# Retention and a gated feed-forward layer on one core: loads queued ahead of transposes, and fences by halves of the outputs

## The chip, the cores and the metric

The kernel runs on one core of one Trainium2 chip. The metric is the device time of one execution in microseconds (us); lower is better. The core has five engines that run side by side: TensorE (PE; its weight loads are listed apart as PEld), VectorE (DVE), ScalarE (ACT), GpSimd (POOL) and SyncE (SP), which here issues nearly all DMAs. TensorE multiplies a moving operand by weights that were loaded before and writes to PSUM, eight banks of accumulators; ScalarE and VectorE bring the results from there to SBUF.

## The reference

For each of 8 batches and 8 heads (sequence 576, head width 64) it computes retention, which is attention without softmax, with a decay that depends on the distance. The heads are laid side by side to 512 columns, and 4608 rows go through a two-layer network with a gate.

```python
scores = scale * np.matmul(q, k.transpose(0, 1, 3, 2))
Dmat = np.where(rel >= 0, gamma[:, None, None] ** rel[None, :, :], 0.0)
ret = scores * Dmat[None, :, :, :]
attn = np.matmul(ret, v)                      # (8, 8, 576, 64)
...
x = attn.transpose(0, 2, 1, 3).reshape(4608, 512)
h = x @ w_in                                  # 512 -> 2048
g = h * (1.0 / (1.0 + np.exp(-beta * h)))
out = g @ w_out                               # 2048 -> 512
```

The decay is separable, so the kernel puts it into q and v as factors (`gq`, `gv`), and only a triangular mask is left. The inputs are random normal numbers.

## The kernel before

**Blocks.** The first 512 rows of each batch form a block (m = 0 to 7); the last 64 rows of all eight batches form a ninth block, "the tails". A block goes up (L714: 16 groups of 4 matmuls with 512 columns, 512 to 2048 wide), through the gate (L718, L719, L721) and down: blocks 0 to 3 with plain matmuls (`down`, L824), blocks 4 to 8 with seven products in place of eight (`seven_mm`, L751).

**Retention of a batch, from batch 2 on.** The 512 rows are taken in half tiles of 64 rows. `scores` (L550) multiplies k by q inside the half tiles and masks the result with VectorE into R. States are sums of k times v over a half tile (`four_states`, L523); `fold` (L528) adds them up and casts them to bf16 into seven tiles `sbq`. `outputs4` (L589) multiplies v by R into four PSUM tiles O4[x, y], 64 matmuls. `crosses4` (L607) adds what earlier half tiles contribute: q times the sums `sbq[e - 1]` for e = 1 to 7, for each of four head pairs p = 2y + pp, and for two heads j in each: 56 matmuls into the same four PSUM tiles. Then `out` (L626) copies O4 to `xT`, the input of the block's up matmuls. `both4` is outputs and crosses together. The tails have the same steps in `tail_scores`, `tail_outputs`, `tail_crosses` (L647 to L698), with 64 outputs and 64 crosses. `XB`, 2, is the first batch done in this way; batches 0 and 1 use larger tiles.

**Small matmuls on TensorE.** All of these work on 64x64 tiles: half of the array's rows and half of its columns, so four quarters. The row half is that of the partitions the weights and the moving operand lie in (`row_d(j)` or `half(x)`, rows 0 to 63 or 64 to 127), the column half that of the PSUM partitions written. In a cross the row half is j and the column half j ^ y. `paired` (L493) takes two lists and issues an entry of each in turn, so that the stream alternates between row halves. `mm` (L498, the matmul is L499) issues all of them.

**The fence.** Within a bank, accumulating matmuls from different row halves must not run together. The crosses therefore come in two parts: first those in which row half j writes the tiles x = j, whose outputs came from the same row half, and then those with x = 1 - j. Before the second part starts, all outputs have to be done: `fence` (L504) has ScalarE make a tiny copy (`fenced`, L505) that waits for the last output matmul, and the first cross of the second part waits for that copy (`after`). In batches 3 to 6 the states of the next batch's first four half tiles (32 matmuls, `ahead`) stand between the two parts.

**Order.** Nothing is scheduled automatically. `fill` is a list of units, mostly one group of four 512-column matmuls each. `streams` are lists of (place, step), and `merged` (L844) issues each step just before the fill unit of that number. `base[n]` is the place of the first unit of block n, `d0` that of the first down unit, `u1` that of block 1's first up unit. A step's instructions go to their engines' queues in this order, each engine works its queue in order, and a step at a wrong place waits there with all that stands behind it.

**Loads and transposes.** SyncE's queue holds q loads (L86, two per batch), k and v loads (`load_kv`: L100, L102, L105, one tile of 128 rows each; L105 in two halves), the DMA transposes of q (`x_q`), of k (`x_k`) and of the tails (all L362), and the stores of the results (L790, L815, L837; L815 are block 0's and 1's, held back and sent by `release`). `pre_q` and `pre` have GpSimd scale q and v and cast k to bf16; a transpose waits for that. A batch has four k/v tiles c = 0 to 3; `x_k(b, 0)` turns the keys of c = 0 and 1, `x_k(b, 1)` those of c = 2 and 3. `kvn` has six buffers, `qs` one. `pair_prep` (L965) says where the loads and the preparation of a pair of tiles stand: for batches 3 to 7 it puts loads of c = 2 and 3 at `at - 28` and `at - 26` (batch 3: `at - 25.4`, `at - 25.3`), among the transposes of the same batch; for batch 2 the streams at L944 to L959 do.

Of the kernel before, what the change touches and what calls it, by code (L numbers as in the profile page):

```python
# [19 lines left out]
def kernel(  # L20
# [15 lines left out]
    P = 128  # L36
# [4 lines left out]
    CB = MB // P  # L41
    PC = P // CB
    TL = S - MB
# [241 lines left out]
    def F(f, *a):  # L285
        return lambda: f(*a)  # L286
# [199 lines left out]
    def row_d(j):  # L486
        return slice(j * D, (j + 1) * D)
# [101 lines left out]
    def outputs4(b):  # L589

        i0 = b * CB
        O4, opened = new_O4(i0, [P, 2, CB, 2 * PC]), set()
        R = batch[b]["R"]

        def one(x, y, cc, pp, kind, hh):
            p, c = 2 * y + pp, 2 * cc + x
            w = cc * PC + kind * PC // 2
            mm(O4[x, y][row_d(hh), pp, :, w:w + PC // 2], live[i0 + tile_of(c, kind)]["vn"][half(x), 2 * p + hh, :],
               R[cc][half(x), hh ^ y, kind, p, :].rearrange("k (i s) -> k i s", i=CB), start=(x, y, hh) not in opened, stop=False)
            opened.add((x, y, hh))  # L600

        for y in range(2):
            paired(*[[F(one, x, y, cc, pp, kind, hh ^ x) for cc in range(2) for pp in range(2) for kind in range(2)
                      for hh in range(2)] for x in range(2)])
        batch[b]["O4"] = O4, fence()

    def crosses4(b, later=None):  # L607

        i0 = b * CB
        O4, after = batch[b]["O4"]  # L610

        def cross(j, e, y, pp, after):
            p, c, kind = 2 * y + pp, e // 2, e % 2
            w = c // 2 * PC + kind * PC // 2
            mm(O4[c % 2, y][row_d(j ^ y), pp, :, w:w + PC // 2], sbq[e - 1][row_d(j), p, :],
               q_cols(i0 + c, row_d(j), p, kind)[0], after=after)

        def crosses(j, x, after=None):
            return [F(cross, j, e, y, pp, after) for e in range(1, 2 * CB) if e // 2 % 2 == x for pp in range(2) for y in range(2)]

        ahead, bank = ([], []), None
        if b < B - 1 and b != XB:
            bank = state_banks()
            ahead = four_states(b + 1, 0, bank)
        paired(*[crosses(j, j) + ahead[j] + crosses(j, 1 - j, None if j else after) for j in range(2)])
        def out(n, x, y, O):  # L626
            to = xt(b)[:, 2 * y:2 * y + 2].rearrange("k p i (c x s) -> k (p i) c x s", c=2, x=2)[:, :, :, x, :]
            e = nc.scalar.copy if n == 1 or b > XB and n % 2 or later is not None else nc.vector.tensor_copy
            e(to, O[:].rearrange("k p i (c s) -> k (p i) c s", c=2))  # L629

        outs = [F(out, n, x, y, O) for n, ((x, y), O) in enumerate(O4.items())]
        if later is not None:
            casts = []
            if bank:
                fold(b + 1, 0, bank, casts=casts, by=nc.scalar.copy)
            later += outs + casts
            return
        for f in outs:
            f()
        if bank:  # L640
            fold(b + 1, 0, bank)
# [23 lines left out]

    def tail_outputs(i0):

        O4, opened, R = new_O4(i0, [P, 2, NT, TL]), set(), live[i0]["R"]

        def one(x, y, t, pp, hh):  # L670
            p = 2 * y + pp
            mm(O4[x, y][row_d(hh), pp, t, :], live[i0 + t]["vn"][half(x), 2 * p + hh, :],
               R[t // 2][half(x), hh ^ y, t % 2 * HP + p, :], start=(x, y, hh) not in opened, stop=False)
            opened.add((x, y, hh))

        for y in range(2):
            paired(*[[F(one, x, y, t, pp, hh ^ x) for t in range(NT) for pp in range(2) for hh in range(2)]
                     for x in range(2)])
        live[i0]["O4"] = O4, fence()

    def tail_crosses(i0, later):

        O4, after = live[i0]["O4"]

        def cross(j, x, t, y, pp, after):
            p = 2 * y + pp
            mm(O4[x, y][row_d(j ^ y), pp, t, :], ends[2 * t + x][row_d(j), p, :], live[i0 + t]["qkT"][row_d(j), 0, p, half(x)],
               after=after)

        for own in range(2):  # L690
            paired(*[[F(cross, j, j ^ own, t, y, pp, after if own else None) for t in range(NT) for pp in range(2) for y in range(2)]
                     for j in range(2)])
        def out(x, y, O):
            for r in range(2):
                to = xt(B)[:, 2 * y:2 * y + 2].rearrange("k p (a r) (s l x) -> k (p a) r l x s", r=2, l=2, x=2)[:, :, r, :, x, :]
                nc.scalar.copy(to, O[:].rearrange("k p (a l) (r s) -> k (p a) r l s", l=2, r=2)[:, :, r])

        later += [F(out, x, y, O) for (x, y), O in O4.items()]  # L698
# [239 lines left out]
    def second(i):  # L938
        for f in (a_O, lambda j: a_cross(j, False), a_x):
# [7 lines left out]
               [(d0 - 4 + 3.3 * g, F(cast_w_out, g)) for g in range(WG)],  # L947
               [(10.3, F(load_q, 1))] + [(10.3, F(load_kv, CB + n, (j,))) for n, j in keys_first],
               [(10.4, F(load_q, 2))] + [(10.4, F(load_kv, 2 * CB + n)) for n in range(2)],
               [(d0 + 8.6, F(load_kv, 2 * CB + 2)), (d0 + 12.6, F(x_q, XB, 0)), (d0 + 12.7, F(x_q, XB, 1)),  # L950
                (d0 + 13.6, F(x_k, XB, 0)), (d0 + 13.8, F(load_kv, 2 * CB + 3)),
                (base[2] - 4.5, F(release, 4)), (base[2] + 8, F(release, 4))],
               [(d0 + 7, F(pre_q, 1, n)) for n in range(4)] + [(d0 + 12.5, F(pre_q, XB, n)) for n in range(4)] + [(d0 + 11.6, F(t_q, 1, 0)), (d0 + 12.6, F(t_q, 1, 1))],
               [(d0 + 8, F(pre, 4, (0,))), (d0 + 8, F(pre, 5, (0,))), (d0 + 9, F(pre, 4, (1,))), (d0 + 9, F(pre, 5, (1,))),
# [10 lines left out]
    def pair_prep(i, at):  # L965
        b, c = seq[i]
        if b is None:
            if c:
                return [(at - 27, F(load_tail, c)), (at - 20, F(load_tail, c + 1)), (at - 17.5, F(pre, i)),
                        (at - 12, F(pre, i + 1)), (at - 12, F(x_tail, i)), (at - 9.5, F(x_tail, i + 1))]  # L970
            return [(at - 31, F(load_tail, c)), (at - 21.5, F(pre, i)), (at - 21, F(load_tail, c + 1)),
                    (at - 13, F(pre, i + 1)), (at - 12, F(x_tail, i)), (at - 9.5, F(x_tail, i + 1))]
        n, st = full.index(i), []
        if b == XB:
            if c == 0:
                return [(d0 + 13, F(pre, i + x, (0,))) for x in range(2)] + \
                       [(d0 + 14, F(pre, i + x, (1,))) for x in range(2)]
            return [(u1 + 8 + x / 2, F(pre, i + x)) for x in range(2)]
        if c == 0:
            st += [(at - 30, F(load_q, b, (0,)))] + ([(at - 30, F(x_k, XB, 1))] if b == XB + 1 else [])  # L980
            st += [(at - 30, F(load_q, b, (1,)))] + [(at - 20 + x, F(pre_q, b, x)) for x in range(4)]
            st += [(at - 14 + 1.5 * x, F(x_q, b, x)) for x in range(2)]
            return st + [(at - 28, F(load_kv, n)), (at - 26, F(load_kv, n + 1)), (at - 16, F(pre, i)),
                         (at - 15, F(pre, i + 1)), (at - 11.5, F(x_k, b, c // 2))]
        turned_at = asked[b + 1] - 30.1
        st += [(turned_at - 0.4 + 0.1 * x, F(pre, i + x, (0,))) for x in range(2)]
        st += [(turned_at, F(x_k, b, c // 2))] + [(turned_at + 0.1 + 0.1 * x, F(pre, i + x, (1,))) for x in range(2)]
        early = b == XB + 1
        return st + [(at - (25.4 if early else 28), F(load_kv, n)), (at - (25.3 if early else 26), F(load_kv, n + 1))]

    def span(a, n, by=1.0):
        return [a + by * x for x in range(n)]
# [30 lines left out]
    for n in range(1, B):  # L1023
# [3 lines left out]
        b, t = n + 1, base[n]  # L1027
        t0 = t + lead.get(n, 0)
        if n == 1:
            at = [t + 17, base[b] - 8.9]  # L1030
        elif n < SB:
            at = [t + 3, t + 18]
        else:
            at = [t0 - 13, t0 + 2] if n < B - 1 else [t0 - 9.5, t0 - 2.5]
# [5 lines left out]
            streams.append([(at[0], F(group1, b, (0,))), (at[1], F(group1, b, (1,))), (at[1] + 4.4, F(both4, b))])  # L1040
        elif n < SB:
            streams.append([(t + 16, F(first_states, b))] * (b == XB + 1) +
                           [(t + 19, F(group1, b, (0, 1))), (t + 25.9, F(both4, b))])
        elif n == B - 1:
            outs = []
            streams.append([(t0, F(tail_scores, take[0])), (t + 13, F(both_tails, take[0], outs))] +
                           queued([t + 16.3, t + 17.6, t + 20.5, t + 22.5], outs))
        else:
            rest, outs = [], []
            t0 -= behind[n]  # L1050
            streams.append([(t0, F(scores, b, (0, 1), rest))] + queued([t0 + 0.1, t0 + 0.9, t0 + 0.9, t0 + 1.8, t0 + 2.6] + span(t0 + 3.4, 4, 0.9), rest))
            by = t + 14.5 if n == SB else t + 12.8
            streams.append([(by, F(both4, b, outs))] + queued([t + 16.3] * 4 + [t + 17.3, t + 18.3, t + 20.3, t + 20.4][:4 if n < B - 2 else 0], outs))
# [32 lines left out]
```

## Time and profile before

| | |
|---|---|
| three runs | 291.69, 292.61, 293.07 us; median 292.61 |
| the profiled execution | 292.13 us, span 290.4 us, granted TensorE clock 1.00 |
| TensorE matmuls, busy | 280.4 us, 97% of the span |
| DVE, ACT, POOL, busy | 168.4, 172.6, 119.6 us |
| small matmuls L499: sc, st, O | 0.19 to 0.20 us mean length each, overlapping |
| DMA transposes L362 | 28 issues; qT lands 5.4 us after issue, kT 3.7 us (medians) |
| k and v loads | 88 issues, 128 or 256 KB; median 3.7 to 5.8 us to landing |

How to read it: the busy share of an engine tells where there is room, and TensorE has next to none. The length of a single small matmul is its latency, many are in flight at once, so their pace is read from the starts: a group's length less the last one's own, divided by the number of steps. A chain of waits is followed back from the end of the program, at each step to what released it; "issue" is time in which the engine waited for nothing that the profile shows.

### The profile page before, as it was taken

What the parts mean: (1) busy time and instruction counts of PE and PEld (TensorE: products, weight loads), DVE (VectorE), ACT (ScalarE), POOL (GpSimd) and SP (SyncE); (2) the same over time, 40 slices, a digit from 0 to 9 for tenths busy, and PEclk for the clock granted to TensorE, in tenths of its full rate; (3) what the DMA queues carried; (4) which work ended last, traced back from release to release, by engine and by line L of the source; (5) the groups of instructions that cost most, each with busy time, mean ns of one, the idle gap of its engine ahead of it and who ended that gap; (6) DMA issues with size and microseconds to landing.
All of it is one profiled execution on the core that took longest, in us unless ns stands there. A gap on an engine that the chain in (4) does not pass through costs nothing.

```text
span 290.4 us, 8109 instructions
## 1 busy us (share of the span) xinstructions
PE 280.4 (97%) x3357; PEld 171.3 (59%) x3385; DVE 168.4 (58%) x314; ACT 172.6 (59%) x306; POOL 119.6 (41%) x219
## 2 busy tenths in 40 slices
PE   8899999999999999999999999999999999999995
PEld 6554446864544454445554885578557845784584
DVE  6563556804673375405538976986597555642673
ACT  4676646686639895882257725772576156837730
POOL 4765206782565473337349245615389000000000
PEclk9999999999999999999999999999999999999999
DMA  7999999999999999599999979996789130003004
GB/s 211 218 341 386 387 275 227 253 187 194 214 153 258 251 277 189 139 254 175 193 257 217 170 113 257 260 162 142 234 192 169 41 148 3 2 29 116 2 2 142
DMA packets 128884, 54.01 MB, mean 186 GB/s; under 512 B 110400, under 2 KB 121680, under 8 KB 128848
## 3 DMA queue, kind: packets, MB, share of 16 engines
q1 hardware_dynamic: 128816, 53.49, 82.9%
q8 instruction: 26, 0.43, 0.7%
q14 instruction: 10, 0.08, 0.1%
q10 hardware_dynamic: 32, 0.01, 0.0%
HBM read 36.71 MB, written 9.44 MB: 159 GB/s over the span
## 4 chain that ended last, share of the span: by engine, by line
PE 86%; SPq 6%; DMA 4%; issue 1%; DVE 1%; POOL 1%; ACT 0%; DVEq 0%; POOLq 0%
PE ph L714 39%; PE po L824 16%; PE U L751 9%; PE Z L751 6%; PE W L751 6%; SPq L100 3%; PE O L499 3%; DMA wt<-in_moe_w_in_dram 3%; PE ph L806 2%; DMA kvn<-in_k_dram 2%; PE sc L499 1%; PE st L499 1%; SPq L198 1%; PE sc L403 0%; DVE sum L535 0%
## 5 line engine op out<-in xcount | busy, mean ns | idle before, releaser
L714 PE MATMUL ph<-xT,w_in_sb 128*128 128x512 bf16 (+1 forms) x544 | 113.9, 363 | 1.4 <-issue 0.6
L721 ACT ACTIVATE gT<-ph,beta_sb 128x512 bf16<-128x512 f32 (+1 forms) x100 | 63.6, 644 | 42.1 <-PE ph L714 41.2
L714 PEld LDWEIGHTS <-w_in_sb 128*128 128x128 bf16 x560 | 53.5, 98 | 55.7 <-POOL w_in_sb L206 0.9
L824 PE MATMUL po<-w_out_sb,gT 128*128 128x512 bf16 x246 | 56.2, 379 | 1.2 <-issue 1.0
L354 POOL CAST kn<-kvn 128x128 bf16<-128x128 f32 (+2 forms) x80 | 30.2, 411 | 58.1 <-DMA kvn<-in_k_dram 57.7
L751 PEld LDWEIGHTS <-sa 128*128 128x128 bf16 x400 | 39.2, 98 | 4.5
L719 DVE TENSOR_SCALAR gT<-hs,ratio 128x512 bf16<-128x512 f32 x40 | 23.8, 594 | 29.1 <-ACT hs L718 28.9
L824 PEld LDWEIGHTS <-gT 128*128 128x128 bf16 x256 | 24.2, 98 | 27.8
L317 POOL TENSOR_TENSOR qs<-qn,gq 128x256 bf16<-128x256 f32 (+1 forms) x36 | 27.5, 792 | 23.3 <-DMA qn<-in_q_dram 14.8
L328 POOL TENSOR_TENSOR vn<-kvn,gv 128x512 bf16<-128x512 f32 x32 | 34.4, 1079 | 4.9 <-DMA kvn<-in_v_dram 4.4
L718 ACT ACTIVATE hs<-ph,beta_sb 128x512 f32<-128x512 f32 x40 | 27.5, 687 | 14.4 <-PE ph L714 13.8
L735 DVE TENSOR_TENSOR sa<-gT 128x1024 bf16<-128x1024 bf16 (+1 forms) x45 | 33.9, 792 | 1.1 <-PE Z L751 0.9
L286 DVE TENSOR_TENSOR R<-sc,late 128x512 bf16<-128x512 f32 x24 | 15.3, 680 | 22.3 <-PE sc L499 12.1
L751 PE MATMUL Z<-b,sa 128*128 128x256 bf16 x160 | 19.1, 273 | 0.0
L751 PE MATMUL U<-b,sa 128*128 128x256 bf16 x160 | 19.1, 273 | 0.0
L248 DVE TENSOR_TENSOR b<-wt 128x512 bf16<-128x512 f32 x20 | 13.8, 736 | 7.1 <-ACT b L244 7.1
L751 PEld LDWEIGHTS <-gT 128*128 128x128 bf16 x160 | 15.6, 98 | 2.9
L407 DVE TENSOR_TENSOR R<-sc,causal 128x512 bf16<-128x512 f32 x16 | 10.2, 686 | 4.6 <-PE sc L403 4.5
L806 PE MATMUL ph<-xT,w_in_sb 128*128 128x512 bf16 x54 | 12.3, 379 | 0.3 <-ACT xT L460 0.2
L809 ACT ACTIVATE gT<-ph,beta_sb 128x512 bf16<-128x512 f32 x14 | 8.6, 686 | 4.2 <-PE ph L806 4.2
L831 ACT COPY ot<-po 128x512 f32<-128x512 f32 x12 | 7.0, 583 | 6.8 <-PE po L824 6.7
L629 ACT CAST xT<-O 128x512 bf16<-128x512 f32 x17 | 8.8, 597 | 2.5 <-PE O L499 2.5
(117 smaller groups left out, 294.4 us busy)
## 6 DMA issues: line engine op xcount, KB each, us to landing
qn<-in_q_dram SPq DMA_DIRECT2D x16, 512.0 KB, 5.4
out_dram<-ot SPq DMA_DIRECT2D x32, 256.0 KB, 3.3
kvn<-in_k_dram SPq DMA_DIRECT2D x20, 256.0 KB, 5.8
kvn<-in_v_dram SPq DMA_DIRECT2D x20, 256.0 KB, 5.6
wt<-in_moe_w_out_dram SPq DMA_DIRECT2D x8, 512.0 KB, 9.0
kvn<-in_k_dram SPq DMA_DIRECT2D x24, 128.0 KB, 4.1
kvn<-in_v_dram SPq DMA_DIRECT2D x24, 128.0 KB, 3.7
wt<-in_moe_w_in_dram SPq DMA_DIRECT2D x5, 512.0 KB, 8.7
```

The costliest lines, as they stand in the source:

```text
L286: return lambda: f(*a)
L317: nc.gpsimd.tensor_tensor(batch[b]["qs"][:, cs, to], q_tiles[b][:, hs, cs].rearrange("p h i d -> p i h d"), gq[:, cs, hs].unsqueeze(3).to_ ...
L328: nc.gpsimd.tensor_tensor(live[i]["vn"][:], kv_tiles.pop(i)[:, 1], gains(gv, row_of(b, c)), ALU.mult)
L354: nc.gpsimd.tensor_copy(kn[:, c % 2, to], t[:, 0, hs])
L714: nc.tensor.matmul(ph, w_in_sb[:, ko, fo * P:(fo + 1) * P], xts[m][:, ko, :, w], start=(ko == 0), stop=(ko == KO - 1))
L718: nc.scalar.activation(h, ph, ACT.Silu, scale=beta_sb[:, fo:fo + 1])
L719: nc.vector.tensor_scalar(gts[m][:, fo], h, ratio[:, fo // 2:fo // 2 + 1], None, ALU.mult)
L721: nc.scalar.activation(gts[m][:, fo, :, w], ph, ACT.Silu, scale=beta_sb[:, fo:fo + 1])
L735: nc.vector.tensor_tensor(sums_a[0][:, held_in[j], ks], quarter(m, *x, ks), quarter(m, *y, ks), op)
L751: nc.tensor.matmul(chains[c, n][:, 0 if alone else p], a, sevens[k // 2][:, j - 1, k % 2, :], start=j in (3, 4, 1) and k == 0 and (alone o ...
L806: nc.tensor.matmul(phs[f][:], w_in_sb[:, ko, f * P:(f + 1) * P], xts[m][:, ko], start=(ko == 0), stop=(ko == KO - 1))
L824: nc.tensor.matmul(po[:, :nn], gT[:, fo, ms, :], w_out_sb[:, fo, n0:n0 + nn], start=(fo == 0), stop=(fo == FO - 1))
```

## The change

Five edits. (1) `outputs4` and `tail_outputs` put a fence behind each half (y = 0, y = 1) of the outputs instead of one behind all; a cross of the second part waits for the fence of its own y. (2) The lists of the crosses run over y outermost instead of innermost. (3) Batch 2's loads of the tile c = 3 move ahead of its q and k transposes; batches 3 to 7 have the loads of c = 2 and 3 at `at - 29.3` and `at - 29.2`. (4) Batch 2's first scores come one fill unit later. (5) Batch 3's outputs and crosses come one fill unit later.

```diff
 def outputs4(b):
-        O4, opened = new_O4(i0, [P, 2, CB, 2 * PC]), set()
+        O4, opened, fences = new_O4(i0, [P, 2, CB, 2 * PC]), set(), []
...
         for y in range(2):
             paired(*[[F(one, x, y, cc, pp, kind, hh ^ x) for cc in range(2) for pp in range(2) for kind in range(2)
                       for hh in range(2)] for x in range(2)])
-        batch[b]["O4"] = O4, fence()
+            fences.append(fence())
+        batch[b]["O4"] = O4, fences
 def crosses4(b, later=None):
...
-               q_cols(i0 + c, row_d(j), p, kind)[0], after=after)
+               q_cols(i0 + c, row_d(j), p, kind)[0], after=after and after[y])
 
         def crosses(j, x, after=None):
-            return [F(cross, j, e, y, pp, after) for e in range(1, 2 * CB) if e // 2 % 2 == x for pp in range(2) for y in range(2)]
+            return [F(cross, j, e, y, pp, after) for y in range(2) for e in range(1, 2 * CB) if e // 2 % 2 == x for pp in range(2)]
 def tail_outputs(i0):
-        O4, opened, R = new_O4(i0, [P, 2, NT, TL]), set(), live[i0]["R"]
+        O4, opened, R, fences = new_O4(i0, [P, 2, NT, TL]), set(), live[i0]["R"], []
...
-        live[i0]["O4"] = O4, fence()
+            fences.append(fence())
+        live[i0]["O4"] = O4, fences
 def tail_crosses(i0, later):
...
-               after=after)
+               after=after and after[y])
 
         for own in range(2):
-            paired(*[[F(cross, j, j ^ own, t, y, pp, after if own else None) for t in range(NT) for pp in range(2) for y in range(2)]
+            paired(*[[F(cross, j, j ^ own, t, y, pp, after if own else None) for y in range(2) for t in range(NT) for pp in range(2)]
                      for j in range(2)])
...
-               [(d0 + 8.6, F(load_kv, 2 * CB + 2)), (d0 + 12.6, F(x_q, XB, 0)), (d0 + 12.7, F(x_q, XB, 1)),
-                (d0 + 13.6, F(x_k, XB, 0)), (d0 + 13.8, F(load_kv, 2 * CB + 3)),
+               [(d0 + 8.6, F(load_kv, 2 * CB + 2)), (d0 + 12.5, F(load_kv, 2 * CB + 3)), (d0 + 12.6, F(x_q, XB, 0)), (d0 + 12.7, F(x_q, XB, 1)),
+                (d0 + 13.6, F(x_k, XB, 0)),
 def pair_prep(i, at):
...
-        early = b == XB + 1
-        return st + [(at - (25.4 if early else 28), F(load_kv, n)), (at - (25.3 if early else 26), F(load_kv, n + 1))]
+        return st + [(at - 29.3, F(load_kv, n)), (at - 29.2, F(load_kv, n + 1))]
...
         if n == 1:
-            at = [t + 17, base[b] - 8.9]
+            at = [t + 18, base[b] - 8.9]
...
-                           [(t + 19, F(group1, b, (0, 1))), (t + 25.9, F(both4, b))])
+                           [(t + 19, F(group1, b, (0, 1))), (t + (26.7 if n == 2 else 25.9), F(both4, b))])
```

The number of matmuls and of DMAs stays the same; ScalarE has seven more copies `fenced`. The order of instructions on VectorE and GpSimd does not change. On SyncE's queue the transposes of a batch stand behind all its k and v loads; before, L362 of q stood between them.

## The prediction

> **What bounds the kernel now.** I read the page first (busy time, clock), then TensorE's waits after 24 us, then the chain of waits through each group of small retention matmuls, then the timeline of single groups, and last SyncE's queue.
>
> ```profile
> PE 280.4 (97%) x3357; PEld 171.3 (59%) x3385; DVE 168.4 (58%) x314; ACT 172.6 (59%) x306; POOL 119.6 (41%) x219
> ...
> PEclk9999999999999999999999999999999999999999
> ```
>
> TensorE is busy 97% of the span at the full granted clock; every other engine is under 60%. What TensorE itself waited for, from 24 us on (total, times, longest):
>
> ```profile
> PE po L824 <- issue: 1.0, 6, 0.2
> PE ph L714 <- issue: 0.6, 4, 0.2
> PE st L499 <- POOL vn L328: 0.4, 1, 0.4
> ```
>
> The ten "issue" pieces of 0.16 us follow groups of small matmuls and stay. So in 266 us only 0.44 us is a wait on another engine that this list shows (before the state matmuls at 109.53, for vn). Whatever lengthens TensorE's stream lengthens the span one for one; there is almost no slack to take it up. Some waits sit ahead of weight loads and show in the chain only, here batch 2's outputs and crosses (start, length, what):
>
> ```profile
> 79.11 0.79 PE O L499 x64
> 79.91 0.02 issue
> 79.93 0.20 ACT fenced L505
> 80.13 0.04 issue
> 80.17 0.45 PE O L499 x32
> ```
>
> ScalarE's fence holds TensorE from 79.90 to 80.17. The same chain at batch 7 has it from 217.00 to 217.27, at the tails from 245.54 to 245.59. Batches 3 to 6 have 32 state matmuls of the next batch between the two halves of the crosses, and no fence on the chain.
>
> **Part 1, fences by halves.** All three fence waits can go: 0.27 + 0.27 + 0.05 = 0.59 us. The first fence can then run while the y = 1 outputs do, and the second is asked for only in the middle of the later crosses. Bounds: 0 (the last fence still ends late) to 0.59; I take 0.59, since the cover, the crosses themselves, gets longer in part 2. The seven added ScalarE copies (0.19 us each, mean of L505) cost nothing: ScalarE is 59% busy, and behind the second fence stand the same instructions as behind the one before.
>
> **Part 2, the new order of the crosses.** This is in the same lines of the diff and is the term that decides. `paired` issues one matmul of row half j = 0, one of j = 1, and so on; a cross of half j writes the column half j ^ y. Before, y ran innermost: the stream went over the four 64x64 quarters of the array in turn, (0,0) (1,1) (0,1) (1,0). Now y runs outermost: (0,0) (1,1) (0,0) (1,1) for 6 or 8 pairs, and only then (0,1) (1,0). Two quarters work, two rest. What a quarter can do, from rows of before:
>
> ```profile
> 47.40 0.40 PE L403 MATMUL sc<-qT,kT 64*128 64x128 bf16 x8
> ...
> 245.07 0.36 PEld L499 LDWEIGHTS <-end 64*64 64x64 bf16 x32
> 245.58 0.33 PEld L499 LDWEIGHTS <-end 64*64 64x64 bf16 x32 [0.15 <-ACT fenced L505]
> ...
> 162.75 1.75 PE U L751 x16
> ```
>
> The last line is the whole array: 1.75/16 = 109 ns for 256 columns, 0.427 ns a column. The first is two row halves in turn, 128 columns each: (0.40 - 0.22 for the last one's own length)/3 steps = 60 ns a pair, about the 128 x 0.427 = 55 ns that one matmul streams. So two tiles give two matmuls in one streaming time, not more. The middle lines are the tails' crosses over four quarters, 64 columns: (0.36 - 0.10)/31 = 8.4 ns a matmul before the fence, (0.33 - 0.10)/31 = 7.4 behind it, where the fence had let a backlog build up. A pair took 16.8 and 14.8 ns, mean 15.8, and one quarter came round every 4 x 7.4 = 30 ns at the best.
>
> After: a pair cannot beat one quarter's own turn. Lower bound 64 x 0.427 = 27 ns, from the columns; the best round seen is 30; the slower round is 4 x 8.4 = 34. If the next weights could not come in under the same quarter's matmul, another 27 on the 30: 57. I take 30, the nearest row. Extra per pair: 30 - 15.8 = 14 ns; bounds 27 - 16.8 = 10 and 57 - 15.8 = 41.
>
> How many pairs: crosses run over e = 1..7, two pp, two y, so 12 + 16 = 28 for each half j. Batches 2 and 7: 28 pairs each. Batches 3 to 6: the halves stand 4 places apart around 16 states, so 32 pairs hold at least one cross, and that one sets the pair's time. Tails: 32. Sum 56 + 128 + 32 = 216. Cost 216 x 14 = 3.0 us; bounds 216 x 10 = 2.2 and 216 x 41 = 8.9. No row of before shows 64-column matmuls on two quarters only, hence the bounds.
>
> The Trainium skill (page "TensorE: Matmul & The Clock Gate", section "Part 3: Packing small matmuls — row/col tiling") says that a weight load runs under a matmul in flight only when their row groups differ. By that rule a pair would be matmul plus load, the 57 ns case. The rows at 245.07 speak against it: with two quarters in each row half and a load and a matmul every 8.4 ns, loads do run beside matmuls of their own row half.
>
> **Part 3, batch 3's outputs a unit later (n == 2).** One fill unit is four 512-column matmuls, 0.86 us. The 0.44 us wait for vn at 109.53 has to be met by a step that comes 0.86 us later, while vn hangs on loads issued at 101.86 behind stores that are not moved. Gain 0.44 (bounds 0 to 0.44). The four matmuls moved ahead fill the time; batch 3's xT copies, done by 111.6, have until 115.55, when its up units start.
>
> **Part 4, loads ahead of transposes.** On SyncE a transpose waits for GpSimd (the queue's own waits: 18.1 us for kn, 17.6 for vn), and the loads stood behind it:
>
> ```profile
> 58.76 3.79 SPq L362 DMA_TRANSPOSE qT<-qs  x2
> 62.66 2.08 SPq L362 DMA_TRANSPOSE kT<-kn  x1
> 64.79 1.29 SPq L105 DMA_DIRECT2D kvn<-in_k_dram  x2
> 66.12 1.31 SPq L105 DMA_DIRECT2D kvn<-in_v_dram  x2
> ...
> 69.47 1.25 SPq L362 DMA_TRANSPOSE kT<-kn  x1
> ```
>
> Batch 2 is the tight one. Four loads of 2.6 us go first, so its transposes start at 61.3; with the shortest issue of L362, 1.23 us, three end at 65.2 against 64.74 now (they waited for GpSimd anyway). The first kT landed 4.0 us after its issue, at 66.6; with 512 KB more ahead of it at some 250 GB/s (the slices' rates) up to 2 us later, 67.1 to 68.9. The scores asked for it at 68.00; a unit later, at 68.86. So that delay covers the move: 0, bound up to 0.5. The second kT landed at 74.76 just as its scores began at 74.89; its loads leave some 6 us earlier, so it comes earlier; TensorE showed no wait there, so nothing is gained. Batches 3 to 7: q and first k transposes come up to 2.6 us later than now, with 9 us to spare at batch 5 (scores at 149.71, first issue 131.8); the second k transposes, which are last (batch 5 lands 144.78 + 3.3 = 148.1 for 149.71), depend on the earlier loads and gain slack. What follows on the queue (stores, the next batch's q) stands behind as many DMAs as before. Cost 0, gain 0.
>
> **Sum.** 3.0 - 0.59 - 0.44 = +2.0 us. The profiled execution took 292.13 us (span 290.4 and 1.7 around it), so 294.1; it lies 0.48 under the median of the three runs, 292.61, on which the same sum gives 294.6. I forecast 294.4.
>
> **Rivals.**
> (a) The order costs nothing: the pace of 8.4 ns is that of the instruction stream, and two quarters keep it. For it: 8.4 ns is a very even pace, and 4 x 7.4 shows that there was some reserve. Against it: the L403 row, where two tiles give one streaming time a pair. Then fences and vn remain: 292.61 - 1.03 = 291.6, not slower. The point that decides: a pair under 15.8 + 1030/216 = 20.6 ns makes the change a gain, and 27 ns of columns do not fit under that.
> (b) Weights of a quarter load only after its matmul: 8.9 - 1.03 = +7.9, so 300.5. Against it the rows at 245.07, with four quarters alone. The skill's rule above gives this case.
> (c) Batch 2's transposes land behind 68.86 and TensorE stands there 0.5 to 1 us on top: 295.1 to 295.6. For it: SyncE's queue loses 2.6 us ahead of them. Against: the present waits for GpSimd swallow most of that.
>
> **How the numbers follow.** Forecast 0.76, (a) 0.13, (b) 0.05, (c) 0.06. The forecast's own bounds: 2.2 - 1.03 = +1.2 and, with rounds of 34 ns, 216 x (34 - 15.8) = 3.9, less 1.03, +2.9; on 292.1 and 292.6 that is 293.3 to 295.5. The range 292.6 to 296.2 takes in (c) and noise, and leaves out (a) and (b), 0.18. 0.5% is 1.46 us, about what a measurement of this kernel can tell from no change. Slower: 0.67 of the forecast (0.09 of it falls under the bound), (b) and (c): 0.78. Same: 0.09 and half of (a): 0.16. Faster, (a) with a little more than I count: 0.06.
>
> **What would show it.** In the chain, batch 2's group from its outputs to the next down matmul now lasts 80.62 - 79.11 = 1.51 us; I expect no L505 in it and about 0.53 + 28 x 0.030 + 0.2 = 1.6. Batches 3 to 6 (161.78 - 160.28 = 1.50) should show about 1.95. The groups of crosses in the timeline should pace at 15 ns a matmul. No vn wait before the states of batch 3, no wait at batch 2's first scores. The forecast is wrong if crosses still start every 8 ns, or if TensorE gains a wait on DMA kT or qT.

## The result, and the profile after

| | before | after |
|---|---|---|
| median, us (22 runs each, side by side) | 292.51 (291.69 to 293.10) | 293.12 (292.42 to 295.70) |
| ratio of the times | 1 | 1.0028, 95% interval 1.0016 to 1.0041 |
| the profiled execution, us | 292.13, span 290.4 | 293.13, span 291.4 |

The change makes the kernel slower by 0.6 us (medians) to 0.8 us (ratio), 0.5 to 1.2 by the interval. The direction was forecast, the size was not: +2.0 us, to 294.4. The 293.1 us lie in the forecast's range of 292.6 to 296.2, but only because its lower end was set down to take in noise; the forecast's own bounds were 293.3 to 295.5.

The page of the changed kernel, the rows of busy time and of the clock:

```profile
PE 281.0 (96%) x3357; PEld 172.1 (59%) x3385; DVE 166.9 (57%) x314; ACT 173.8 (60%) x313; POOL 119.3 (41%) x219
...
PEclk9999999999999999999999999999999999999999
```

TensorE is the bound as before, with the same matmuls at the same clock; ScalarE has its seven copies more. What TensorE's matmuls waited for from 24 us on (total, times, longest):

```profile
PE po L826 <- issue: 1.0, 6, 0.2
PE ph L716 <- issue: 0.6, 4, 0.2
PE sc L499 <- DMA kT<-kn: 0.3, 1, 0.3
```

The wait for vn is gone (edit 5) and a wait for kT stands in its place. The chain of waits shows it at batch 2's first scores:

```profile
66.05 3.13 DMA kT<-kn
69.18 0.04 issue
69.22 0.45 PE sc L499 x32
```

and SyncE's queue why (start, length, what):

```profile
58.54 2.15 SPq L105 DMA_DIRECT2D kvn<-in_k_dram  x2
60.74 1.31 SPq L105 DMA_DIRECT2D kvn<-in_v_dram  x2
62.21 3.73 SPq L362 DMA_TRANSPOSE qT<-qs  x2
66.05 1.28 SPq L362 DMA_TRANSPOSE kT<-kn  x1
```

The first kT was issued at 62.66 before and at 66.05 now, 3.4 us later behind the loads; it landed at 69.18, and the scores, one unit later than before, wanted it 0.3 us sooner.

The chain through batch 2's outputs and crosses has no fence any more:

```profile
78.82 0.65 PE po L826 x3
79.47 1.54 PE O L499 x114
81.01 0.16 issue
81.17 0.81 PE po L826 x3
```

But 81.01 - 79.47 = 1.54 us, against 80.62 - 79.11 = 1.51 before: the 0.27 us of the fence are not gained, they are used up. Batches 3 to 6 take 1.71 to 1.86 us in the chain, where 1.95 was expected; the 1.50 named as their length before was that of batch 5 alone, batch 4 had 1.78. The tails show more. Of the timeline of weight loads, after:

```profile
245.80 0.23 PEld L499 LDWEIGHTS <-vn 64*64 64x64 bf16 x16
245.96 0.95 PEld L499 LDWEIGHTS <-end 64*64 64x64 bf16 x64
```

64 loads of crosses in one stretch: (0.95 - 0.10)/63 = 13.5 ns a cross, 27 a pair, where the two rows before the change (245.07 and 245.58) paced at 8.4 and 7.4 ns with a pause between them. The 27 ns are not yet the price of a pair, since waits for the two fences are in them: by the starts of the single matmuls the pairs of one run come every 31 to 32 ns, as forecast, but the runs overlap. The second run (it begins with kT) starts among the last pairs of the first (they have qT):

```profile
246.11 0.20 PE L499 MATMUL O<-qT,end 64*64 64x64 bf16 x2
246.12 0.22 PE L499 MATMUL O<-kT,end 64*64 64x64 bf16 x2
246.14 0.22 PE L499 MATMUL O<-qT,end 64*64 64x64 bf16 x3
246.17 0.20 PE L499 MATMUL O<-kT,end 64*64 64x64 bf16 x2
```

It starts 0.16 us after the first run, 20 ns for each of that run's 8 pairs. ScalarE, before and after, at the same place:

```profile
244.67 0.69 ACT L721 ACTIVATE gT<-ph,beta_sb 128x512 bf16<-128x512 f32 x1 [0.17 <-PE ph L714]
245.34 0.19 ACT L505 COPY fenced<-lscale 128x2 f32<-128x2 f32 x1
```

```profile
245.54 0.69 ACT L723 ACTIVATE gT<-ph,beta_sb 128x512 bf16<-128x512 f32 x1 [0.17 <-PE ph L716]
246.12 0.41 ACT L505 COPY fenced<-lscale 128x2 f32<-128x2 f32 x2
```

The two fences stand back to back in one row (x2, 0.41 us). The first starts only as the gate (L723, 245.54 + 0.69) runs out; the second goes after the first. The first output started at 244.56 and 245.43; so the last fence ended 245.53 - 244.56 = 0.97 us after it before, and 246.53 - 245.43 = 1.10 now. Splitting the fence made the last one 0.13 us later. In batch 2 no gate is in the way, and ScalarE is idle between the two copies:

```profile
79.91 0.19 ACT L505 COPY fenced<-lscale 128x2 f32<-128x2 f32 x1 [0.89 <-PE O L499]
80.33 0.19 ACT L505 COPY fenced<-lscale 128x2 f32<-128x2 f32 x1 [0.23 <-PE O L499]
```

The second still starts 0.93 us after the first output (79.40), where the single fence starts after 0.88 in the kernel before and after 0.85 in e3, e10 and e11, which have the old fence too. Between the copies the trace has an instruction that waits for a semaphore (17 ns), which the single fence does without; what makes up the rest of the 0.05 to 0.08 us is open.

For the whole kernel the cleanest measure is the stretch from the first to the last start of a cross in a group, fence included, taken from the starts of the single matmuls. The experiments below are in the same table (us):

```
crosses and fences              batch 2   batch 7   tails
kernel before                    0.828     0.791    0.745
fences by halves alone (e2)      0.892     0.839    0.864
new order alone (e1)             0.972     0.944    0.895
changed kernel                   0.888     0.864    0.865
changed kernel, old order (e9)   0.893     0.840    0.864
mixed order, halves (e12)        0.889     0.861    0.866
```

In these three places the change costs 0.06 + 0.07 + 0.12 = 0.25 us (0.28 against e3, whose fence and order are the old ones). What ends them is the last fence. From its end to the start of the last cross it takes 0.30 to 0.31 us with one fence and the old order, 0.45 with one fence and the new order (e1), and 0.29 to 0.30 in all 15 groups with a split fence (changed kernel, e2, e8, e9, e12), whatever the order. So the new order costs nothing behind a split fence, and the split fence's own lateness is what is left. In batches 3 to 6 the stretch also holds 32 states; without pauses over 0.3 us (those are waits for vn) the four together take 3.6 to 4.1 us in the seven profiles with the old order (before, e2, e3, e9 to e12; mean 3.80) and 4.0 to 4.5 in the three with the new (e1, e8, after; mean 4.24): +0.4 us, from single profiles that scatter by as much.

### The profile page after: what moved, and what is told of

The parts are those of the page before. It is cut to its first block, busy times and chain, and to the rows that moved or that the text cites. A ratio compares the mean times of both kernels' runs of the same rounds, so it can differ in the third digit from the quotient of the medians.

```text
span 291.4 us, 8126 instructions
## 1 busy us (share of the span) xinstructions
PE 281.0 (96%) x3357; PEld 172.1 (59%) x3385; DVE 166.9 (57%) x314; ACT 173.8 (60%) x313; POOL 119.3 (41%) x219
## 4 chain that ended last, share of the span: by engine, by line
PE 74%; DMA 10%; SPq 10%; POOL 2%; issue 1%; DVE 0%; POOLq 0%
PE ph L716 33%; PE po L826 14%; PE U L753 9%; SPq L100 8%; PE W L753 6%; PE Z L753 6%; PE O L499 4%; DMA wt<-in_moe_w_out_dram 3%; DMA qn<-in_q_dram 2%; DMA wt<-in_moe_w_in_dram 2%; PE sc L499 2%; DMA kvn<-in_k_dram 2%; PE st L499 1%; SPq L86 1%; DMA kT<-kn 1%
## 5 line engine op out<-in xcount | busy, mean ns | idle before, releaser
L723 ACT ACTIVATE gT<-ph,beta_sb 128x512 bf16<-128x512 f32 (+1 forms) x100 | 63.7, 645 | 42.1 <-PE ph L716 41.3
L354 POOL CAST kn<-kvn 128x128 bf16<-128x128 f32 (+2 forms) x80 | 29.5, 402 | 32.5 <-DMA kvn<-in_k_dram 32.2
L721 DVE TENSOR_SCALAR gT<-hs,ratio 128x512 bf16<-128x512 f32 x40 | 22.0, 550 | 29.9 <-ACT hs L720 29.4
L328 POOL TENSOR_TENSOR vn<-kvn,gv 128x512 bf16<-128x512 f32 x32 | 33.7, 1058 | 6.7 <-DMA kvn<-in_v_dram 3.3
L248 DVE TENSOR_TENSOR b<-wt 128x512 bf16<-128x512 f32 x20 | 14.4, 770 | 6.4 <-ACT b L244 6.4
L342 POOL TENSOR_TENSOR kn<-tln,gq 128x128 bf16<-128x128 f32 (+1 forms) x6 | 3.9, 648 | 16.0 <-DMA tln<-in_q_dram 16.0
```

What stands on the lines that cost most here:

```text
L328: nc.gpsimd.tensor_tensor(live[i]["vn"][:], kv_tiles.pop(i)[:, 1], gains(gv, row_of(b, c)), ALU.mult)
L354: nc.gpsimd.tensor_copy(kn[:, c % 2, to], t[:, 0, hs])
L721: nc.vector.tensor_scalar(gts[m][:, fo], h, ratio[:, fo // 2:fo // 2 + 1], None, ALU.mult)
L723: nc.scalar.activation(gts[m][:, fo, :, w], ph, ACT.Silu, scale=beta_sb[:, fo:fo + 1])
```

## The experiments

Two theories at the start. A: the order of the crosses costs, at a pair's price of 10 to 14 ns, and the fences give part of it back. B: the moved loads and places cost, and the order is free. Runs of the kernel before on the same chip stand beside each set of runs; ratios are to those.

**One part alone.** e1 takes the order only, e2 the fences only, e3 the moves only ("..." marks lines left out; the tails' functions are changed in the same way).

```diff
 e1
-            return [F(cross, j, e, y, pp, after) for e in range(1, 2 * CB) if e // 2 % 2 == x for pp in range(2) for y in range(2)]
+            return [F(cross, j, e, y, pp, after) for y in range(2) for e in range(1, 2 * CB) if e // 2 % 2 == x for pp in range(2)]
...
 e2
...
+            fences.append(fence())
+        batch[b]["O4"] = O4, fences
...
-               q_cols(i0 + c, row_d(j), p, kind)[0], after=after)
+               q_cols(i0 + c, row_d(j), p, kind)[0], after=after and after[y])
...
 e3
+               [(d0 + 8.6, F(load_kv, 2 * CB + 2)), (d0 + 12.5, F(load_kv, 2 * CB + 3)), (d0 + 12.6, F(x_q, XB, 0)), (d0 + 12.7, F(x_q, XB, 1)),
...
+        return st + [(at - 29.3, F(load_kv, n)), (at - 29.2, F(load_kv, n + 1))]
...
+            at = [t + 18, base[b] - 8.9]
...
+                           [(t + 19, F(group1, b, (0, 1))), (t + (26.7 if n == 2 else 25.9), F(both4, b))])
```

> Only the order of the crosses (y outermost) is changed in the kernel before; one fence as before. Theory A (a pair of crosses on two quarters takes about 27 ns in place of some 17, as the tails' 64 crosses show in the trace of the changed kernel: 0.87 us in place of 0.53 without the fence's gap): 216 pairs x 9 to 11 ns = 1.9 to 2.4 us, less what the longer first part hides of the three fence gaps (about 0.1 us each) and of four junctions (0.05 each): +1.3 to +1.9 us. Theory B (the order is nearly free, the loss comes from the moved loads and scores): +0.3 us or less.

> Only the fences by halves, the crosses in the old order, in which the second cross of the second part already asks for the second fence. Theory A: within 0.2 us of before, since the last output matmul still decides. Rival (the earlier fence lets enough matmuls go ahead): the three gaps of 0.32, 0.30 and 0.22 us shrink by half, -0.4 us.

> Only the moved loads, batch 2's first scores and batch 3's outputs a unit later; fences and order of the crosses as before. Theory A: the wait for vn before batch 3's states goes (-0.44 us), the wait for kT at batch 2's first scores comes (+0.3 to +0.4 us): -0.5 to +0.2 us. Theory B (the loss sits here): +0.6 us or more.

Measured (before: 292.73): e1 293.50 us, ratio 1.0037 (1.0012 to 1.0061); e2 292.80, 1.0004 (0.9984 to 1.0024); e3 292.82, 0.9999 (0.9979 to 1.0020). Only the order's cost is clear of noise by itself, and e2 and e3 come out as their A has them; B, which gave the order 0.3 us at most, falls narrowly. The intervals of e2 and e3 still leave room for up to 0.7 us each. e1's 1.1 us (0.35 to 1.8) are a little under what A expected, and not all need be the order's: the chain of its profile has a pause of 1 us in batch 5.

```profile
158.63 1.77 POOL kn L354 x3
160.41 0.18 issue
160.58 1.22 POOL vn L328
161.80 0.04 issue
161.84 0.19 PE st L499
```

The states of the next batch wait for its vn. e2 has the same pause, 0.8 us at the same state; the profile of before has none. It hangs on the place of the loads (e10). How many executions of e1 or of the kernel before have it is not known. For e2 the table says more than the time: the split fence alone makes the crosses longer in all three places, by 0.06, 0.05 and 0.12 us.

**The outputs on two quarters.** Were two quarters always 14 ns dearer, the outputs would show it too.

```diff
-            paired(*[[F(one, x, y, cc, pp, kind, hh ^ x) for cc in range(2) for pp in range(2) for kind in range(2)
-                      for hh in range(2)] for x in range(2)])
+            paired(*[[F(one, x, y, cc, pp, kind, hh ^ x) for hh in range(2) for cc in range(2) for pp in range(2)
+                      for kind in range(2)] for x in range(2)])
```

> The kernel before, with the outputs' loops turned so that the head half hh runs outermost: 16 pairs on two quarters, then 16 on the other two, in each y half; crosses and fences as before, results the same. It repeats the suspected cost on other matmuls: 7 groups x 32 pairs. Theory A: 224 x (27 to 32 - 16) ns = +2.5 to +3.6 us, each group of 64 outputs 0.9 to 1.0 us in place of 0.54. Theory B: 0 to +0.3 us.

293.26 us, ratio 1.0012 (0.9991 to 1.0033): a miss, at most 1 us where 2.5 to 3.6 were expected. The edit makes runs of 8 pairs, not of the 16 that the expectation names. The starts say why so little is lost. In a run of 8 pairs on two quarters the pairs come every 32 ns, but when the stream goes over to the other two, their first matmuls start in between the last ones of the old run. From the first output to the last cross the groups grew by 0.12 us in batch 2 (1.38 to 1.50), 0.13 in batch 7 and 0.18 in the tails: 4 to 6 ns for each of 32 pairs.

**A pair's price by itself.** This made a new rival: is the price set by the length of the run? Three kernels issue every cross three times (their outputs are not the reference's) in the old order, in the new one with 18 to 24 pairs in a run, and in the new one with runs of 6 or 8.

```diff
 e5
+            return [F(cross, j, e, y, pp, after) for rep in range(3) for e in range(1, 2 * CB) if e // 2 % 2 == x for pp in range(2) for y in range(2)]
...
 e6
+            return [F(cross, j, e, y, pp, after) for y in range(2) for rep in range(3) for e in range(1, 2 * CB) if e // 2 % 2 == x for pp in range(2)]
...
 e7
+            return [F(cross, j, e, y, pp, after) for rep in range(3) for y in range(2) for e in range(1, 2 * CB) if e // 2 % 2 == x for pp in range(2)]
...
```

> The kernel before with every cross issued three times in the old order (the list of each part run through three times; the outputs are not the reference's). 56 pairs more in each of the batches 2 to 7 and 64 more in the tails, 400 in all, and nothing of fences, loads or places changed, so this prices a pair by itself. All theories: 16 to 17 ns a pair on four quarters, 6.4 to 6.8 us over the kernel before, 299.3 us. It is the base for the two runs beside it.

> The same crosses three times, y outermost and the repeats inside it, so that 18 to 24 pairs in a row use the same two quarters. Theory A (a quarter takes 31.7 ns a turn, and only the ends of a run of 6 or 8 pairs overlap with work on the other two quarters): near 31 ns for each added pair, 12.4 us more than the new order alone (293.5), 305.9 us. Theory B (two quarters really pace at the some 26 ns net that the changed kernel's groups show, at any length): 10.4 us more, 303.9 us.

> The same crosses three times, the whole list of the new order run through three times, so that the runs on two quarters stay at 6 or 8 pairs. Theory A: each change of quarters lets the first matmuls of the next run start under the last of this one, so an added pair costs what it does in the changed kernel, some 26 ns: 10.4 us more than the new order alone, 303.9 us, and about 2 us less than with long runs. Theory B: the same as with long runs. If each pair costs the predicted 30 ns whatever the run's length, both stand at 305.5 us.

Measured (before: 293.40): 322.78, 323.78 and 328.83 us, ratios 1.097, 1.099 and 1.120. All three expectations missed by 18 to 25 us, because TensorE stood still for 1.6 to 4.6 us in six places of each, which none of the theories had; the last section is about that. The times therefore say nothing of the pair, but the stretches between the pauses do. The tails' weight loads, in e5, e6 and e7:

```profile
275.94 1.00 PEld L499 LDWEIGHTS <-end 64*64 64x64 bf16 x105
278.97 0.79 PEld L499 LDWEIGHTS <-end 64*64 64x64 bf16 x87 [2.03 <-issue]
```

```profile
271.33 1.56 PEld L499 LDWEIGHTS <-end 64*64 64x64 bf16 x105
274.35 1.37 PEld L499 LDWEIGHTS <-end 64*64 64x64 bf16 x87 [1.45 <-issue]
```

```profile
276.01 1.19 PEld L499 LDWEIGHTS <-end 64*64 64x64 bf16 x105
279.33 1.07 PEld L499 LDWEIGHTS <-end 64*64 64x64 bf16 x87 [2.13 <-issue]
```

Less the last load's own 0.10 us and over the steps, 104 and 86, times two for a pair: old order 17.3 and 16.0 ns, long runs 28.1 and 29.5, short runs 21.0 and 22.6. Theory A's point on the length holds: a long run on two quarters costs the predicted 30 ns, a run of 6 or 8 pairs some 22. At the length that the change uses, a pair is dearer by 4 to 7 ns.

**Batch 2's loads back behind its transposes**, all else as changed:

```diff
-               [(d0 + 8.6, F(load_kv, 2 * CB + 2)), (d0 + 12.5, F(load_kv, 2 * CB + 3)), (d0 + 12.6, F(x_q, XB, 0)), (d0 + 12.7, F(x_q, XB, 1)),
-                (d0 + 13.6, F(x_k, XB, 0)),
+               [(d0 + 8.6, F(load_kv, 2 * CB + 2)), (d0 + 12.6, F(x_q, XB, 0)), (d0 + 12.7, F(x_q, XB, 1)),
+                (d0 + 13.6, F(x_k, XB, 0)), (d0 + 13.8, F(load_kv, 2 * CB + 3)),
```

> The changed kernel with batch 2's loads of c = 3 put back behind its transposes; all else as changed. Theory A (the wait for kT at batch 2's first scores, 0.37 us longer than before in the group's span, comes from these loads ahead of the transposes): no kT wait, the group back at about 1.2 us, 0.3 to 0.4 us less than the changed kernel, 292.8 us. Theory B (the wait comes with the later place of the scores or from GpSimd): the wait stays and the time is that of the changed kernel, 293.1 us.

The chain at the place of the kT wait:

```profile
67.02 1.73 PE po L826 x8
68.74 0.37 PE sc L499 x32
```

The scores follow the down matmuls without a gap; kT had landed at 66.85. A's mechanism is shown. The time, 293.08 us, ratio 1.0004 (0.9977 to 1.0031), is too wide to show 0.3 us; the span of its profile is 290.6, against 291.4.

**The order undone in the changed kernel.** e9 is the changed kernel with y innermost again.

> The changed kernel with the old order of the crosses (y innermost); fences by halves, the loads and both later places stay. Theory A (the order is the only part that costs; by the starts of the crosses it adds 1.8 us in the changed kernel): the second half's fence is waited for again, some 0.3 us each in batches 2 and 7 and the tails, and the time is 0.9 to 1.4 us below the changed kernel, ratio to the kernel before 0.998 to 0.9995. Theory B (the loss comes from the moved loads, the order is paid back by the fences): the same as the changed kernel, ratio 1.003.

292.49 us beside 292.09, ratio 1.0012 (1.0000 to 1.0024): halfway between the theories, and the interval holds neither. Against the changed kernel's 1.0028 undoing the order gave back about 0.0016, 0.5 us, though the two intervals overlap. The table has the reason that it was not 0.9 to 1.4: in batches 2 and 7 and the tails the order makes little or no difference once the fence is split (0.893, 0.840, 0.864 against 0.888, 0.864, 0.865). Behind the second fence there stand either 8 pairs at 31 ns or 16 at 16, the same quarter of a microsecond, and that fence sets the end. (e8, with the new order, has 0.935 in batch 7; there the second fence itself came 0.07 us later, and the crosses behind it took the same 0.30 us.)

**Toward a faster kernel.** e10 moves only the loads of batches 3 to 7, e11 adds batch 3's later outputs, e12 adds split fences and y outermost only behind a fence:

```diff
 e12
+        halves = b == B - 1 or b == XB
...
+            if halves and x != j:
+                return [F(cross, j, e, y, pp, after) for y in range(2) for e in es for pp in range(2)]
+            return [F(cross, j, e, y, pp, after) for e in es for pp in range(2) for y in range(2)]
...
```

> The kernel before with the loads of c = 2 and 3 of batches 3 to 7 moved ahead, nothing else. Theory A (where these loads stand behind the transposes, the vn of the next batch's first tiles is finished 1.2 us before or up to 1 us after the states of batch 5 ask for it, and in some executions TensorE waits there): no wait for vn at batch 5, vn done some 4 us before it is asked for, and a gain of 0.2 to 0.5 us, ratio 0.998 to 0.9993. Theory B (as the prediction had it, nothing is gained): ratio 0.9995 to 1.0005, and the vn wait before the states of batch 3 stays at 0.4 us or more.

> The kernel before with the loads of batches 3 to 7 moved ahead and batch 3's outputs and crosses a unit later; batch 2, fences and order as before. Theory A: the vn waits of batches 3 and 5 are both gone and no wait for kT comes in; 0.5 to 0.9 us below the kernel before, ratio 0.997 to 0.9985. Theory B (TensorE's queue takes up such waits elsewhere): within 0.1 us of the kernel before.

> As the run with the loads of batches 3 to 7 and batch 3 a unit later, with fences by halves, and with y outermost only in the second part of the crosses of batches 2 and 7 and of the tails, where a fence was waited for; all other crosses keep y innermost. Theory A: the second part starts at once on its y = 0 crosses, and 12 to 16 pairs at 10 ns more (0.15 us) take the place of a gap of 0.23 to 0.33 us: three times 0.1 us less than without it, 0.7 to 1.2 us below the kernel before, ratio 0.996 to 0.9976. Theory B (the gap only moves to the y = 1 crosses): the same as without it.

Measured (before: 292.09): e10 292.03 us, ratio 0.9994 (0.9980 to 1.0008); e11 292.15, 0.9997 (0.9981 to 1.0014); e12 292.29, 1.0002 (0.9991 to 1.0014). None beats the kernel before by what can be measured: e10's interval holds both of its theories, e11 falls short of its A by its median, e12 by its whole interval. e10's mechanism is there: GpSimd's row of vn for batch 5's turn,

```profile
153.99 1.04 POOL L328 TENSOR_TENSOR vn<-kvn,gv 128x512 bf16<-128x512 f32 x1
```

is done at 155.03, where e1 had it at 161.80 and the kernel before at 159.76, for states that ask for it at about 161. Its wait for vn at batch 3 is 0.2 us and not 0.4 (waits of the matmuls), so that e11 had only 0.2 us left to win there. For e12, A falls: its three places stand at 0.889, 0.861 and 0.866, as with any split fence and longer than with a single one.

## Why the prediction was right and wrong

The step that failed most is the sum of part 2, "Cost 216 x 14 = 3.0 us": every pair was charged the full turn of a quarter, and the order cost about 0.5 us. The gain of part 1, 0.59 us, did not come either, which by itself would have made the kernel slower than forecast.

**The bound** was right: TensorE stays at 96 to 97%, nothing else came near, and what lengthened its stream lengthened the span (290.4 to 291.4).

**Part 1, fences by halves** (forecast -0.59 us, measured about +0.25 together with the order in the three places, +0.23 in e2 by itself). The step that failed is "the seven added ScalarE copies cost nothing: ScalarE is 59% busy". The busy share is not the question. In batch 7 and the tails the first copy stands directly ahead of the second in an in-order queue, at the one moment that counts, and behind a gate activation of 0.69 us that keeps it from going early; in batch 2 ScalarE is idle between them, and the second copy is late all the same, by 0.05 to 0.08 us. The bounds were wrong with it: 0 to 0.59 left out a loss, since only the old fence's lateness was considered, and not that the new last fence could be later than the old one (by 0.13 us in the tails). The thought that the longer crosses of part 2 would cover the fence was right in part: set against e1, which has the new order and one fence, the split gained 0.19 us in the three places. The wait at the tails was also read too small, 0.05 us in the chain, where the starts of the crosses show a gap of 0.23.

**Part 2, the order** (forecast +3.0, at least +2.2; measured about +0.5 beside the split fence, and +1.1, 0.35 to 1.8, by itself in e1). The turn of a quarter was right: pairs of one run come every 31 to 32 ns, and in long runs a pair costs 28 to 29.5. The rule built on it, that no pair can beat that turn, failed for short runs. Two terms were mis-sized. A pair was put at 14 ns more, as if every run were long; in runs of 6 or 8 it is 4 to 7, because the next run starts under the end of the last. And it was charged at all 216 pairs, 88 of them in places where the end is set by the second fence and the order is hidden: a gain of the fences and a cost of the order, added up as two terms, were one wait. What is left is 128 pairs in batches 3 to 6 at 3 to 4 ns; 8 of the 32 in each batch are a cross beside a state, which no run here prices apart. Rival (a), that the order costs nothing, falls with e1, and its mechanism with the 31 ns. Its point, 20.6 ns a pair, is about what short runs take; below it the change was to be a gain, and it was none because the gain in the fences was not there.

**Rival (b)**, weights that load only after their quarter's matmul, 57 ns a pair, is excluded: two quarters with 18 to 24 pairs in a run paced at 28 to 29.5 ns. The rule of the Trainium skill that gave it (page "TensorE: Matmul & The Clock Gate", section "Part 3: Packing small matmuls — row/col tiling": loads overlap matmuls in flight only when the row groups differ) does not agree with this trace, where a pair every 28 to 29.5 ns leaves no time for a load apart from a matmul of the same rows; the same section also lets a load into the background weight buffer go ahead of matmuls in flight, and with that the trace agrees.

**Part 3, batch 3 a unit later** (-0.44): the wait for vn before its states is gone in the profiles of after and of e3. That it shortened the time is not shown: e11 against e10 gave nothing that can be measured.

**Part 4, the loads** (forecast 0; measured about +0.3, and a gain of perhaps 0.2). Rival (c) came in part: kT landed at 69.18 for an estimated 67.1 to 68.9 and stopped TensorE for 0.3 us, less than the 0.5 to 1 of the rival. The prediction had named a wait for kT as a sign against itself. The step that failed is the queue's timing: the transposes were to start at 61.3 and end by 65.2, at the shortest issue of L362; they started at 62.21, the two of q took 3.73 us, and the one of k ended at 67.33. "Gain 0" for batches 3 to 7 was read from one execution. There vn came 1.2 us ahead of need; in e1 and e2, with the loads in the same places, it came 0.6 to 0.8 us late, and with the loads moved it came 4 to 5 us early (156.88 in the changed kernel, for 161.3).

**The sum**: +0.25 and +0.4 to 0.5, less 0.44, plus 0.3, is +0.5 to +0.6, less up to 0.2 for the vn of batch 5; measured +0.6 to +0.8, interval 0.5 to 1.2. The parts come from single profiles and are known to some 0.2 us each.

## What to carry to other kernels

A wait that is removed and a slowing that is added at the same place are one term: write down what ends the stretch afterwards, and charge only what lies on that. When a synchronising instruction is split in two, both go through the same in-order queue; look at what stands ahead of the first at that moment, not at the engine's busy share, and expect the second to come later than the single one did (here by 0.05 to 0.13 us). And before a wait is called absent, see with how much margin its producer was done: with about 1 us it came and went here between profiles whose loads stood in the same places.

## What the runs showed of the hardware

**Small matmuls seem to outrun the instruction supply.** The runs with every cross three times had pauses that no semaphore explains. The waits of e5's matmuls:

```profile
PE O L499 <- issue: 16.2, 5, 4.4
PE st L499 <- issue: 2.6, 1, 2.6
```

In e5, e6 and e7 alike the six pauses stand behind 861, 1371, 1881, 2264, 2774 and 3797 matmuls, whatever the order and the pace; the distances are multiples of 127.5 to 127.9 matmuls, or 255 instructions with their weight loads. The profile's pages count instruction packets, before and in e5:

```profile
q8 instruction: 26, 0.43, 0.7%
```

```profile
q8 instruction: 33, 0.54, 0.7%
```

0.54 MB over 33 is 16 KB a packet, and 2 x 4185 TensorE instructions over 33 are 254 to a packet, the same as the distance between pauses. So, it seems, TensorE comes to the end of a packet before the next has arrived: 128 small matmuls with their loads take 1.1 us in the old order, and two packets' worth of them in a row (232 to 264 small matmuls a group in these kernels, 120 to 152 in the original) leave no time to fetch. In batch 2 of e5 the packet's transfer began 0.8 us after the last matmul had started and the pause lasted 3.3 us. In all 18 pauses of the three runs TensorE went on 1.2 to 1.7 us after an instruction packet's transfer had ended. The Trainium skill (page "Runtime: NRT & Kernel Launch", section "Instruction fetch mechanics") has blocks of 16 KiB, 256 instructions, which agrees, and says that crossing one is mostly hidden; here it cost up to 4.6 us. That fetching is the cause is inferred from the counts and these times; no run here varied it alone. The kernel before and the changed one show no such pause.

**The clock fell behind the pauses.** e7's row of the granted clock:

```profile
PEclk9999999999799989999799799979999999799999
```

Each of its six dips begins within 1.5 us of the end of one of the six pauses; the granted clock was 0.969 over that execution. The pauses of e7 sum to 18.0 us and 400 pairs at 22 ns to 8.8; the span grew by 326.9 - 290.4 = 36.5, and 0.031 of 326.9, 10.1 us, is about the rest. Not every pause has a dip: e5 has them behind four and e6 behind one, and pauses of 2.9 and 3.0 us in e6 have none. What decides is open.

**Matmuls do not start in the order of the program across quarters.** In the tails of e4 the first crosses start at 246.59 us, the last of the outputs issued before them at 246.68, and in the changed kernel runs overlap in the same way (the rows at 246.11 to 246.17). This is what makes short runs on two quarters cheap: 21 to 22.6 ns a pair in e7, and 28.1 to 29.5 in e6, where only the length of the runs differs.
